# Attention over the tail of a KV cache on one core: unit 5's K is turned in later slots, and two weight loads change places

## The chip, the core and the metric

The kernel runs on one core of a Trainium2 chip. The core has engines that run side by side, each through its own instructions in order: TensorE (PE, with its weight loads shown apart as PEld), VectorE (DVE), ScalarE (ACT), GpSimd (POOL) and SyncE (SP), which here issues the loads. An instruction that needs another engine's result waits for a semaphore, and everything behind it on the same engine waits too. The metric is the device time of one execution in microseconds.

## The reference

Eight sequences, each with 32 new positions, 32 query heads and 4 KV heads. Of the cache only the last W = 2048 positions are used.

```python
W = min(4096, max(256, Sk // 4))          # Sk = 8192, so W = 2048
q = (x @ wq).reshape(B, Sq, Hq, Dh).transpose(0, 2, 1, 3)
k = jnp.repeat(k_cache[:, :, Sk - W:, :], rep, axis=1)
v = jnp.repeat(v_cache[:, :, Sk - W:, :], rep, axis=1)
p = softmax(einsum("bhqd,bhkd->bhqk", q, k) * Dh ** -0.5)
o = einsum("bhqk,bhkd->bhqd", p, v)
return o.transpose(0, 2, 1, 3).reshape(B, Sq, Hq * Dh) @ wo
```

x is 8 x 32 x 1024, wq 1024 x 4096, wo 4096 x 1024, a head is 128 wide; all is bfloat16.

## The kernel before

**Units and slots.** The work is cut into 32 units, one for each pair of KV head (group g) and sequence b, eight units to a group, in the order of the groups. A unit has 2048 keys and 256 query rows (8 heads x 32 positions). It is done in four chunks of 512 keys, and a chunk of a unit is a *slot*: unit 0 has slots 0 to 3, unit 5 has slots 20 to 23, and so on to slot 127. The loop in `run` (L452 to L485) writes into every engine's queue, slot by slot: the scores S = K Q^T of this chunk on PE (L464), the exponential on ACT (L466), the product P·V of the chunk two slots earlier on PE (L475), then side work. At the end of a unit `finish_unit` divides by the row sums and turns the result, on DVE (L412 to L419). At a unit's start DVE copies the loaded V into one of three tiles va whose rows hold V and a column of ones (L406); P·V reads that tile. The order is written by hand: each engine runs its instructions as they are emitted, and no scheduler moves them.

**Three ways to K^T.** PE needs K with the head dimension on the partitions. Units 0 to 4 (`PE_T`): K is loaded as it is, PE transposes it (L231, two pieces to a half, in the four slots of the unit before) and DVE copies each half out of PSUM (L233). Units 5, 8, 11, ... 29 (`V_T`): K is loaded as it is; DVE transposes 32 x 32 blocks of it into a tile kb, in four instructions (L246, "blocks"), and sixteen moves put the quarters in their places in kTv. POOL makes the moves (L256); for unit 5 one in four is made by DVE (L254). A move takes one 32-partition quarter of kb over all sixteen key tiles, so it needs all four blocks, and the scores need all sixteen moves. All other units: the DMA transposes on the way in (L193).

**Side work and its slots.** `side_plan` (L423) makes a list of pieces for each slot: the projections of Q for the next groups (`Q_SLOTS`, L270), the output projection (`O_SLOTS`, L290), and blocks and moves of the `V_T` units. An entry of `V_T` names the unit after whose loads K is loaded, the slots of the blocks, the first slot of the moves, the slot that they end before, and how many of sixteen moves are POOL's. `spread` deals pieces evenly over a range of slots. In a slot these pieces come last, after the copies of K_T pieces.

**Loads.** SP issues them in one queue. Units 2 and 3 are loaded in `start`, units 4 to 7 in slot 8, and unit u from 8 on in slot 4(u-5). `load_unit` (L202) issues K and V of a unit, then K of a `V_T` unit that is due there, and then the weights whose entry in `W_AT` names the unit. The weights are a list of 28 half-pieces of 512 KB; its first four are wq of group 1 (two halves of two), numbers 4 to 7 are wq of group 2. Eight loads can be on their way at a time: the next waits for the one eight places before it.

Of the kernel before, what the change touches and what calls it, by code (L numbers as in the profile page):

```python
# [21 lines left out]

PE_T = (0, 1, 2, 3, 4)

V_T = {5: (2, (5, 6, 8, 10), 10, 17, 12),
       **{u: (u - 4, range(4 * u - 16, 4 * u - 12), 4 * u - 13, 4 * u - 4, 16) for u in (8, 11, 14, 17, 20, 23, 26, 29)}}
W_AT = (3, 3, 4, 4, 8, 8, 9, 9, 11, 12, 13, 13, 14, 15, 16, 16, 18, 19, 19, 20, 22, 22, 23, 24, 25, 26, 28, 28)

Q_SLOTS = {1: (17, 31), 2: (38, 54), 3: (69, 83)}
O_SLOTS = {0: (54, 71), 1: (84, 101), 2: (99, 123), 3: (124, 143)}  # L30
# [71 lines left out]
class Fast:  # L102
# [72 lines left out]
    def load_k(self, ui, part=None):  # L175
# [3 lines left out]
        src = self.k_cache[b, g, self.Sk - self.W:, :]  # L179
        if ui not in V_T and ui not in self.kT:  # L180
            self.kT[ui] = self.ktp.tile([P, KT, P], BF16, name="kT")
        if ui in PE_T or ui in V_T:
            H = KT // 2
# [18 lines left out]
    def load_unit(self, ui):  # L202

        if ui < len(self.units):
            if ui not in V_T:
                self.load_k(ui, None if ui in PE_T else 0)
            self.load_v(ui, self.nc.sync)
            if ui not in V_T and ui not in PE_T:
                self.load_k(ui, 1)
        for u, at in V_T.items():  # L210
            if at[0] == ui:
                self.load_k(u)
        for p, at in zip(self.weights, W_AT):
            if at == ui:
# [21 lines left out]
    def kv_pieces(self, ui):  # L236
# [11 lines left out]
        def move(k, d):  # L248
# [3 lines left out]
            in_ = st["kb"][k * 32:(k + 1) * 32, :, d * 32:(d + 1) * 32]  # L252
            if d >= V_T[ui][4] // 4:
                nc.vector.tensor_copy(out=out, in_=in_)  # L254
# [168 lines left out]
    def side_plan(self):  # L423

        S = self.B * self.NCH
        plan = {s: [] for s in range((len(self.units) + 8) * self.NCH)}

        def spread(pieces, s0, s1):
            for k, p in enumerate(pieces):
                plan[s0 + (s1 - s0) * k // len(pieces)].append(p)  # L430
        for g, w in Q_SLOTS.items():
            spread(self.q_pieces(g), *w)
        for g, w in O_SLOTS.items():
            spread(self.o_pieces(g, 0) + (self.o_pieces(g, 1) if g < self.Hkv - 1 else []), *w)
        for ui, (_, s0, s1, s2, _) in V_T.items():
            blocks, moves = self.kv_pieces(ui)
            for k, p in enumerate(blocks):
                plan[s0[k]].append(p)
            spread(moves, s1, s2)
        return plan  # L440

# [209 lines left out]
```

## Time and profile before

| | us |
|---|---|
| median of 3 runs | 187.37 (187.13 to 187.44) |
| the profiled execution | 187.37 |
| its span, first to last instruction | 185.6 |
| PE busy in it | 178.8 |
| DVE busy | 115.1 |
| ACT busy | 131.7 |
| POOL busy | 94.7 |

The span is 1.77 us shorter than the time of the execution it belongs to. A row of a timeline has the start in us, the length in us, the engine, the line of the kernel, the operation, output and inputs with their shapes, and how many such instructions are merged; idle time of the engine before the row stands in brackets, with what ended it. Rows of one engine can overlap a little, since an instruction starts before the last has left the pipeline. A list of waits has who waited and for whom, the total in us, how many times, and the longest. A busy engine isn't by itself the bound: what counts is whose work is late for another.

The first loads reach PE at 4.3 us (x) and 6.8 us (the first weights of wq). Slot 4 starts at 18.98 us, slot 8 at 23.44, slot 12 at 27.89, slot 16 at 32.34, slot 20 at 37.65.

### The profile page before, as it was taken

What the parts mean: (1) busy time and instruction counts of PE and PEld (TensorE: products, weight loads), DVE (VectorE), ACT (ScalarE), POOL (GpSimd) and SP (SyncE); (2) the same over time, 40 slices, a digit from 0 to 9 for tenths busy, and PEclk for the clock granted to TensorE, in tenths of its full rate; (3) what the DMA queues carried; (4) which work ended last, traced back from release to release, by engine and by line L of the source; (5) the groups of instructions that cost most, each with busy time, mean ns of one, the idle gap of its engine ahead of it and who ended that gap; (6) DMA issues with size and microseconds to landing.
All of it is one profiled execution on the core that took longest, in us unless ns stands there. A gap on an engine that the chain in (4) does not pass through costs nothing. (4 is left out here: it accounts for less than half of the span.)

```text
span 185.6 us, 5054 instructions
## 1 busy us (share of the span) xinstructions
PE 178.8 (96%) x2048; PEld 153.1 (82%) x2064; DVE 115.1 (62%) x267; ACT 131.7 (71%) x133; POOL 94.7 (51%) x150
## 2 busy tenths in 40 slices
PE   7699999999999999999999999999999999999993
PEld 2589999999999999987878999987777888888842
DVE  0128699994586685586467558647746855445372
ACT  2207899787789777777777677787777888888700
POOL 2000007949939959929954980796299189500000
PEclk9999999999999999999999999999999999999999
DMA  6999999999999999999999999999999999930012
GB/s 151 321 397 415 414 415 389 195 270 353 296 274 304 310 320 398 368 240 254 376 323 250 367 349 276 202 409 357 269 371 329 192 326 174 276 96 0 4 62 62
DMA packets 52507, 51.75 MB, mean 279 GB/s; under 512 B 39424, under 2 KB 40064, under 8 KB 52480
## 3 DMA queue, kind: packets, MB, share of 16 engines
q1 hardware_dynamic: 51904, 50.87, 95.6%
q10 hardware_dynamic: 576, 0.52, 0.8%
q8 instruction: 17, 0.28, 0.6%
q14 instruction: 10, 0.08, 0.2%
HBM read 41.42 MB, written 0.52 MB: 226 GB/s over the span
## 5 line engine op out<-in xcount | busy, mean ns | idle before, releaser
L466 ACT ACTIVATE pT<-s_ps 128x1024 bf16<-128x1024 f32 x128 | 128.9, 1025 | 33.3 <-PE s_ps L464 32.3
L256 POOL TENSOR_SCALAR kTv<-kb 32x512 bf16<-32x512 bf16 x140 | 93.7, 670 | 65.4 <-DMA k_raw<-in_k_cache_dram 27.0
L475 PEld LDWEIGHTS <-pT 128*128 128x128 bf16 x1024 | 68.5, 98 | 3.1
L464 PEld LDWEIGHTS <-kT 128*128 128x128 bf16 x368 | 34.8, 98 | 10.3
L290 PE MATMUL op_ps<-wo_sb,OT 128*128 128x512 bf16 (+1 forms) x120 | 32.8, 365 | 0.8
L270 PE MATMUL q_ps<-xT,wq_sb 128*128 128x256 bf16 x192 | 28.2, 273 | 0.0
L475 PE MATMUL o_ps<-va_112,pT 128*128 128x129 bf16 x352 | 27.1, 220 | 0.0
L475 PE MATMUL o_ps<-va_113,pT 128*128 128x129 bf16 x352 | 27.0, 220 | 0.1
L475 PE MATMUL o_ps<-va_114,pT 128*128 128x129 bf16 x320 | 24.7, 220 | 0.0
L246 DVE STREAM_TRANSPOSE kb<-k_raw 128x512 bf16<-128x512 bf16 x36 | 23.8, 684 | 0.0
L412 DVE RECIPROCAL RL_all<-o_ps 128x2 f32<-128x2 f32 x32 | 5.2, 164 | 27.5 <-PE o_ps L475 27.5
L417 DVE TENSOR_SCALAR o_sb<-o_ps,RL_all 128x128 bf16<-128x128 f32 x64 | 19.5, 346 | 1.1
L464 PEld LDWEIGHTS <-kTv 128*128 128x128 bf16 x144 | 13.9, 98 | 5.1
L270 PEld LDWEIGHTS <-wq_sb 128*128 128x128 bf16 x192 | 17.0, 98 | 1.2
L464 PE MATMUL s_ps<-QT_63,kT 128*128 128x256 bf16 x112 | 16.8, 273 | 0.0
L419 DVE STREAM_TRANSPOSE OT<-o_sb 128x256 bf16<-128x256 bf16 x32 | 14.2, 445 | 1.1
L464 PE MATMUL s_ps<-QT_66,kT 128*128 128x256 bf16 x96 | 14.4, 273 | 0.1
L290 PEld LDWEIGHTS <-OT 128*128 128x128 bf16 x136 | 11.1, 98 | 2.8 <-DVEq L77 0.6
L464 PE MATMUL s_ps<-QT_65,kT 128*128 128x256 bf16 x80 | 12.0, 273 | 0.1
L464 PE MATMUL s_ps<-QT_64,kT 128*128 128x256 bf16 x80 | 12.0, 272 | 0.1
L297 DVE TENSOR_TENSOR oacc<-op_ps,oacc 128x512 f32<-128x512 f32 x8 | 5.5, 682 | 7.4 <-PE op_ps L290 7.4
L406 DVE COPY va_113<-v_sb 128x2048 bf16<-128x2048 bf16 x11 | 9.5, 859 | 0.0
(46 smaller groups left out, 104.0 us busy)
## 6 DMA issues: line engine op xcount, KB each, us to landing
v_sb<-in_v_cache_dram SPq DMA_DIRECT2D x32, 512.0 KB, 7.0
wo_sb<-in_wo_dram SPq DMA_DIRECT2D x16, 512.0 KB, 6.3
wq_sb<-in_wq_dram SPq DMA_DIRECT2D x14, 512.0 KB, 7.1
k_raw<-in_k_cache_dram SPq DMA_DIRECT2D x13, 512.0 KB, 5.7
wq_sb<-in_wq_dram SPq DMA_DIRECT2D x4, 256.0 KB, 7.0
kT<-in_k_cache_dram SPq DMA_TRANSPOSE x36, 6.9
k_raw<-in_k_cache_dram SPq DMA_DIRECT2D x2, 256.0 KB, 8.2
x_sb<-in_x_dram ACTq DMA_DIRECT2D x1, 256.0 KB, 3.7
```

The costliest lines, as they stand in the source:

```text
L246: nc.vector.transpose(out=st["kb"][:, sl, :], in_=self.k_raw[ui][:, sl, :])
L256: nc.gpsimd.tensor_scalar(out=out, in0=in_, scalar1=1.0, scalar2=1.0, op0=ALU.mult, op1=ALU.mult)
L270: nc.tensor.matmul(st["ps"][:, 0:self.NQ], lhsT=self.wq_t[g, i][:, c % (DC // 2), hl * P:(hl + 1) * P], rhs=self.xT[:, c, :], start=(c == ...
L290: nc.tensor.matmul(ps[:, 0:w], lhsT=self.OT[:, gq, c, t * P:(t + 1) * P], rhs=self.wo_t[gq][:, c, n0:n0 + w], start=(k == 0), stop=(k == 7))
L297: nc.vector.tensor_tensor(out=acc, in0=ps[:, 0:w], in1=acc, op=ALU.add)
L406: self.nc.vector.tensor_copy(out=self.va[ui % 3][:, :, 0:self.Dh], in_=self.v_sb[ui][:, :, :])
L412: nc.vector.reciprocal(out=rl[:, ui * QT_N:(ui + 1) * QT_N], in_=o_ps[:, :, Dh])
L417: nc.vector.tensor_scalar(out=o_sb[:, qt, :, :], in0=o_ps[:, qt, 0:Dh].rearrange("p (i c) -> p c i", c=4), scalar1=rl[:, ui * QT_N + qt:ui ...
L419: nc.vector.transpose(out=self.OT[:, g * QT_N:(g + 1) * QT_N, :, b * self.Sq:(b + 1) * self.Sq], in_=o_sb[:, :, :, :])
L464: nc.tensor.matmul(s_ps[:, jj, :], lhsT=self.kT[ui][:, c * CJ + jj, :], rhs=q_u, start=True, stop=True)
L466: nc.scalar.activation(out=pT[:, :, :], in_=s_ps[:, :, :], func=ACT.Exp, bias=0.0, scale=self.scale)
L475: nc.tensor.matmul(o_ps[:, qt, 0:self.VW], lhsT=pT[:, jj, qt * P:(qt + 1) * P], rhs=va[:, j, 0:self.VW], start=(j == 0 and qt == 0), stop= ...
```

## The change

`V_T` gets a range of slots for the blocks in place of a list, in the entry of unit 5 with other numbers. The blocks of unit 5 stood in slots 5, 6, 8 and 10; `spread(blocks, 6, 14)` puts them into 6, 8, 10 and 12. Its moves stood in slots 10 to 16 and now stand in 12 to 16. For the other units of `V_T`, `spread` gives the slots that stood there before. In `W_AT` the first entry goes from 3 to 2, so the first half-piece of wq of group 1 is issued behind K and V of unit 2 and K of unit 5, ahead of K and V of unit 3; and the eighth goes from 9 to 10, so the last half-piece of wq of group 2 is issued behind the loads of unit 10 and K of unit 14.

```diff
-V_T = {5: (2, (5, 6, 8, 10), 10, 17, 12),
-       **{u: (u - 4, range(4 * u - 16, 4 * u - 12), 4 * u - 13, 4 * u - 4, 16) for u in (8, 11, 14, 17, 20, 23, 26, 29)}}
-W_AT = (3, 3, 4, 4, 8, 8, 9, 9, 11, 12, 13, 13, 14, 15, 16, 16, 18, 19, 19, 20, 22, 22, 23, 24, 25, 26, 28, 28)
+V_T = {5: (2, 6, 12, 17, 12),
+       **{u: (u - 4, 4 * u - 16, 4 * u - 13, 4 * u - 4, 16) for u in (8, 11, 14, 17, 20, 23, 26, 29)}}
+W_AT = (2, 3, 4, 4, 8, 8, 9, 10, 11, 12, 13, 13, 14, 15, 16, 16, 18, 19, 19, 20, 22, 22, 23, 24, 25, 26, 28, 28)
@@ side_plan
         for ui, (_, s0, s1, s2, _) in V_T.items():
             blocks, moves = self.kv_pieces(ui)
-            for k, p in enumerate(blocks):
-                plan[s0[k]].append(p)
+            spread(blocks, s0, s1 + (s1 - s0) // 3)
             spread(moves, s1, s2)
```

The rows of V with their ones column are 320 bytes in both kernels (`VA_ROW` = 160).

## The prediction

> **What bounds the kernel now.** I read the page's totals and clock first, then PE's list of waits, then the engines' rows in order of time around the work that the change moves.
>
> ```profile
> PE 178.8 (96%) x2048; PEld 153.1 (82%) x2064; DVE 115.1 (62%) x267; ACT 131.7 (71%) x133; POOL 94.7 (51%) x150
> ...
> PEclk9999999999999999999999999999999999999999
> ...
> PE q_ps L372 <- DMA wq_sb<-in_wq_dram: 1.4, 1, 1.4
> ```
>
> PE is busy for 96% of the span at full clock. Its list of waits has one wait for loaded data, 1.4 us for the first weights, before 7 us. In its rows in order of time no group from 13.65 us to 180 us has idle time before it. So an engine that gets faster in between brings nothing, and only a new hole in PE can change the time there. The question is which results reach PE with little to spare. Unit 5's K^T is one: its scores are PE's first work on a turned K, in slot 20.
>
> ```profile
> 28.59 8.78 POOL L256 TENSOR_SCALAR kTv<-kb 32x512 bf16<-32x512 bf16 x12 [27.02 <-DMA k_raw<-in_k_cache_dram]
> ...
> 37.16 0.37 PEld L270 LDWEIGHTS <-wq_sb 128*128 128x128 bf16 x4
> 37.54 0.43 PEld L464 LDWEIGHTS <-kTv 128*128 128x128 bf16 x4
> ```
>
> POOL makes its twelve moves of unit 5 in one run from 28.59 to 37.37 us. PE loads the first weights from the result at 37.54. The slack is 0.17 us. The idle time before POOL's run is put down to a DMA, but K of unit 5 had landed at 20.94; what came last was the fourth block of L246 on DVE, since every move reads all sixteen tiles of kb:
>
> ```profile
> 22.98 1.28 DVE L246 STREAM_TRANSPOSE kb<-k_raw 128x512 bf16<-128x512 bf16 x2
> 24.19 0.65 DVE L233 COPY kT<-tp 128x1024 bf16<-128x1024 bf16 x1
> 24.77 0.67 DVE L406 COPY va_114<-v_sb 128x2048 bf16<-128x2048 bf16 x1
> 25.36 0.70 DVE L246 STREAM_TRANSPOSE kb<-k_raw 128x512 bf16<-128x512 bf16 x1
> ...
> 27.16 0.65 DVE L233 COPY kT<-tp 128x1024 bf16<-128x1024 bf16 x1
> 27.74 0.69 DVE L246 STREAM_TRANSPOSE kb<-k_raw 128x512 bf16<-128x512 bf16 x1
> 28.35 0.65 DVE L233 COPY kT<-tp 128x1024 bf16<-128x1024 bf16 x1
> 29.03 0.31 DVE L254 COPY kTv<-kb 32x512 bf16<-32x512 bf16 x1
> 29.38 1.04 DVE L406 COPY va_112<-v_sb 128x2048 bf16<-128x2048 bf16 x1
> ```
>
> The fourth block ends at 28.43 and POOL starts 0.16 later. DVE has no idle time from 22.4 to 41.9 us in this listing, so the place of a block in its queue is the time at which it is done.
>
> **The change, part 1: blocks and moves of unit 5.** The blocks go from slots 5, 6, 8, 10 to 6, 8, 10, 12; the moves from slots 10 to 16 into 12 to 16. Nothing is added or removed: four blocks, twelve moves on POOL, four on DVE. In the built program PE's, ACT's and POOL's orders are the same; on DVE the fourth block now stands behind the second kT copy of unit 3 and behind the V copy of unit 3 (va_112), and one move follows it. I walk DVE's queue again with the distances from start to start of the rows above: kT copy 0.58, block 0.62, V copy 0.59.
> - First block 22.98. The second kT copy of unit 2 would start at 23.60, but its transposes on PE end then (23.21 + 0.39), so 23.64; V copy 24.22; second block 24.81 to 25.43.
> - Unit 1's division waits for PE's last product at 25.61, so it starts at 25.65 (25.98 before). Its four instructions take 1.18 (25.98 to 27.16), so the first kT copy of unit 3 is at 26.83, the third block at 27.41.
> - The second kT copy of unit 3 waits for PE's transposes, which end at 28.06: 28.10. V copy of unit 3 28.68. Fourth block 29.27 to 29.96.
> - POOL starts at 29.96 + 0.16 = 30.12, 1.53 later than before.
>
> How long POOL's run takes: an undisturbed move lasts 0.61 with 0.06 before the next, so 12 x 0.61 + 11 x 0.06 = 8.0. Before, 8.78 were taken: one move lasted 0.96 beside the V copy of unit 3, one 0.95 beside that of unit 4 (at 33.89), one 0.70 beside a move on DVE. The first of these is gone, since that copy now lies before POOL's start; the other two stay: 8.0 + 0.34 + 0.09 = 8.45, and the end is 38.57. How soon PE follows POOL no row shows. The nearest is PE behind DVE at the start: the zeroed tile is done at 1.14, the first weight load at 1.19, so 0.05; from DVE to POOL it was 0.16. I take 0.05, the row that ends at PE. The load of unit 5's first K^T goes from 37.54 to 38.62: **a hole of 1.08 us in PE**, 1.53 less the slack of 0.17, less some 0.33 by which POOL's run is shorter, plus the 0.05. PE runs in order, and behind the waiting load stand the P·V of unit 4, Q pieces of group 1 and all later units. They have nothing spare to make it up with, so it stays to the end.
>
> Bounds: POOL undisturbed from 30.0 gives 38.0 and a hole of 0.5; POOL from 30.4 (DVE 0.3 late) with 8.78 and a further 0.3 from DVE's moves gives 39.5 and a hole of 2.0. A gain from this part is excluded: the fourth block can't stand before 29.2, because the kT copy ahead of it waits for PE's transposes.
>
> [...] The row: the V copy of unit 4 alone takes 0.67 (as at 24.77) and lengthened the move beside it by 0.34, not by its whole length. [...] I go by the row.
>
> What else DVE serves in this stretch: the kT copy of unit 4 ends at 32.19 and PE uses it at 32.23. In the new order unit 2's division stands behind the fourth block and one move: 29.96 + 0.03 + 0.31 + 0.04 = 30.34, as before (30.34). At 0.1 late, PE would wait that 0.1 in slot 16 and as much less in slot 20, so it adds nothing. V copy of unit 4: done 34.88, needed 35.44. The first block of unit 8 keeps its place, and POOL's run for unit 8 starts after that unit's fourth block (39.86), after the new end of unit 5's run.
>
> **Part 2: weights.** (a) The first half-piece of group 1's wq goes ahead of K and V of unit 3 in SP's queue, 512 KB. The transfers there land every 1.23 us (K of unit 3 22.16, V 23.40, weights 24.63), so K of unit 3 lands at 23.4 and V at 24.6. PE's transposes of it start at 24.33 with their weight load at 24.23: 0.8 spare where 2.1 were. V of unit 3 is read at 28.7. Cost 0; without the cover, 0.1 for every 0.1 beyond 24.2. Behind them the second half lands where it did, at 26.25. (b) The last half-piece of group 2's wq moves from behind unit 9's K, V to behind unit 10's K, V and K of unit 14. Before it landed at 56.05; the new place in the same queue, filled by the same bytes, is that of K of unit 14, 61.03. SP passes it over a transposing load (the DMA that SP was busy with until 56.03), so the transfers of unit 10 start one transfer sooner. PE reads this half first in slot 39, at 61.25, its third matmul 61.47, which the hole moves to 62.55. Cost 0 with 1.5 spare; bounds 0, and 0.9 if it lands only where the second transfer after it did (63.44).
>
> **Sum.** The profiled execution took 187.37 (span 185.6 and 1.77 around it), which is the median too. 187.37 + 1.08 + 0 + 0 = 188.45.
>
> **Rivals.**
> - The weights of group 2 come late as well. For: DMA falls to 10 to 34 GB/s for about a microsecond near 54.5 us while transposing loads run, and such a dip may now lie just before this half-piece. Against: the queue holds the same bytes. 188.45 + 0.9 = 189.35.
> [...]
> - Not slower: POOL's run fits after all. It would have to end by 37.49, 7.37 after its start, which is the twelve moves at their minimum of 0.607 (7.28) with no pauses. Then PE has no hole: 187.37. Against: pauses of 0.06 stand between all its moves now. It decides only from 0.6 us per move. A real gain would have to come from the first 13 us, where the order of loads is unchanged.
>
> **Chances.** Forecast 0.73, late weights 0.10, longer POOL run 0.08, POOL fits 0.09. The likeliest gives 188.45. The range goes from the lower bound of the hole (0.5, 187.9, less 0.1 for scatter) to the dearer rivals: 187.8 to 189.4. A measurement of this kernel tells about 0.2% (0.37 us) from no change; a hole of 0.5 is above that, so slower takes all but the last case: 0.91, with 0.07 for same and 0.02 for faster.
>
> **What would show it.** Right: POOL's run of twelve starts near 30.1 and ends near 38.6; PE's weight load of kTv in slot 20 waits for POOL about 1.1 us and is the only new wait; the span is some 186.7. Wrong: the run ends before 37.5; a wait of PE on k_raw near 24.2 or on wq_sb near 62; or a slot 20 without a hole and another time nevertheless.

## The result and the profile after

| | before | changed |
|---|---|---|
| median, us | 187.25 (187.13 to 187.44, 6 runs) | 188.31 (187.87 to 188.78, 6 runs) |
| ratio | | 1.0058, 95% interval 1.0041 to 1.0076 |
| the profiled execution, its span | 187.37, 185.6 | 188.31, 186.4 |

The change makes the kernel slower by 1.06 us. The changed kernel's rows around slot 20 show where. First POOL's run of moves for unit 5, then PE's weight loads (start, length, engine, line; in brackets the idle time before):

```profile
30.04 8.37 POOL L256 TENSOR_SCALAR kTv<-kb 32x512 bf16<-32x512 bf16 x12 [28.47 <-PE o_ps L474]
```

```profile
37.03 0.37 PEld L270 LDWEIGHTS <-wq_sb 128*128 128x128 bf16 x4
38.47 0.33 PEld L463 LDWEIGHTS <-kTv 128*128 128x128 bf16 x4 [1.06 <-POOL kTv L256]
```

(Lines of `run` are one less than before: L463 is the scores, L474 is P·V.) POOL starts 1.45 us later than before, its run ends at 38.41, and PE's weight load on kTv, which stood 0.01 us behind the last load on wq before, now stands idle for 1.06 us and starts 0.06 after POOL's end. DVE's rows show why POOL starts so late:

```profile
27.31 0.69 DVE L246 STREAM_TRANSPOSE kb<-k_raw 128x512 bf16<-128x512 bf16 x1
27.97 0.69 DVE L233 COPY kT<-tp 128x1024 bf16<-128x1024 bf16 x1
28.58 0.68 DVE L406 COPY va_112<-v_sb 128x2048 bf16<-128x2048 bf16 x1
29.18 0.70 DVE L246 STREAM_TRANSPOSE kb<-k_raw 128x512 bf16<-128x512 bf16 x1
29.91 0.29 DVE L254 COPY kTv<-kb 32x512 bf16<-32x512 bf16 x1
```

The fourth block stands behind the kT copy and the V copy of unit 3 and ends at 29.88. The bracket of POOL's row names P·V on PE as the releaser, but the block's end is 0.16 before POOL's start, the same distance as before. The V copy takes 0.68 here and took 1.04 before, when POOL's moves ran beside it.

From slot 20 on PE runs without new waits. The list of what its weight loads waited for has one entry that before lacks:

```profile
PEld L463 <- POOL kTv L256: 1.1, 1, 1.1
```

The first scores of unit 5 start 1.05 after the matmul ahead of them, where 0.11 is normal, so PE lost 0.94. From these scores to the last instruction both profiles take 147.9 us, so the loss stays whole. The changed execution had come through its start 0.12 faster (slot 16 at 32.22 against 32.34), which is why the spans differ by 0.8.

### The profile page after: what moved, and what is told of

Read it like the earlier page. It is cut to its first block, busy times and chain, and to the rows that moved or that the text cites. A ratio compares the mean times of both kernels' runs of the same rounds, so it can differ in the third digit from the quotient of the medians.

```text
span 186.4 us, 5054 instructions
## 1 busy us (share of the span) xinstructions
PE 179.0 (96%) x2048; PEld 152.9 (82%) x2064; DVE 116.0 (62%) x267; ACT 131.8 (71%) x133; POOL 94.2 (51%) x150
## 5 line engine op out<-in xcount | busy, mean ns | idle before, releaser
L465 ACT ACTIVATE pT<-s_ps 128x1024 bf16<-128x1024 f32 x128 | 129.0, 1025 | 34.2 <-PE s_ps L463 33.2
L474 PEld LDWEIGHTS <-pT 128*128 128x128 bf16 x1024 | 68.5, 98 | 3.1
L463 PEld LDWEIGHTS <-kT 128*128 128x128 bf16 x368 | 34.8, 98 | 10.3
L474 PE MATMUL o_ps<-va_112,pT 128*128 128x129 bf16 x352 | 27.1, 220 | 0.0
L474 PE MATMUL o_ps<-va_113,pT 128*128 128x129 bf16 x352 | 27.0, 220 | 0.1
L474 PE MATMUL o_ps<-va_114,pT 128*128 128x129 bf16 x320 | 24.7, 220 | 0.0
L463 PEld LDWEIGHTS <-kTv 128*128 128x128 bf16 x144 | 13.8, 98 | 6.2 <-POOL kTv L256 1.1
L463 PE MATMUL s_ps<-QT_63,kT 128*128 128x256 bf16 x112 | 16.8, 273 | 0.0
L463 PE MATMUL s_ps<-QT_66,kT 128*128 128x256 bf16 x96 | 14.4, 273 | 0.1
L463 PE MATMUL s_ps<-QT_65,kT 128*128 128x256 bf16 x80 | 12.0, 273 | 0.1
L463 PE MATMUL s_ps<-QT_64,kT 128*128 128x256 bf16 x80 | 12.0, 272 | 0.1
```

What stands on the lines that cost most here:

```text
L463: nc.tensor.matmul(s_ps[:, jj, :], lhsT=self.kT[ui][:, c * CJ + jj, :], rhs=q_u, start=True, stop=True)
L465: nc.scalar.activation(out=pT[:, :, :], in_=s_ps[:, :, :], func=ACT.Exp, bias=0.0, scale=self.scale)
L474: nc.tensor.matmul(o_ps[:, qt, 0:self.VW], lhsT=pT[:, jj, qt * P:(qt + 1) * P], rhs=va[:, j, 0:self.VW], start=(j == 0 and qt == 0), stop= ...
```

## The experiments

Each kernel is compared with runs of the kernel before on the same chip, whose medians were 187.29 (25 runs), 187.38 (11) and 187.43 (23) in the three groups. "Lost" is the distance from start to start across a hole, less the normal 0.11 us, or less 0.06 ahead of transposes.

**The parts by themselves.** The turn alone:

```diff
-V_T = {5: (2, (5, 6, 8, 10), 10, 17, 12),
+V_T = {5: (2, (6, 8, 10, 12), 12, 17, 12),
```

> The kernel before with the turn of unit 5 alone moved (blocks in slots 6, 8, 10, 12, moves in 12 to 16); the weights stay. Theory (the hole in PE comes from POOL's later run alone): POOL's run starts near 30.1 us against 28.6 and ends near 38.4; PE's first weight load of kTv waits some 1.0 us for it; 0.9 to 1.1 us slower than before, the whole of the change. Rival (the weights bear a part): no more than 0.5 us slower. Second question, the scatter: the changed kernel spread over 0.9 us in six runs, before over 0.3. If the turn makes it, these runs spread over 0.6 us or more.

188.39 us (187.96 to 188.89), ratio 1.005 (1.0033 to 1.0067): the whole of the change. POOL's run is that of the changed kernel to 0.01 us:

```profile
30.04 8.36 POOL L256 TENSOR_SCALAR kTv<-kb 32x512 bf16<-32x512 bf16 x12 [28.47 <-PE o_ps L475]
```

The second question fell away: on this chip the kernel before spread from 186.89 to 187.94 itself, so the scatter isn't the change's.

The weights alone:

```diff
-W_AT = (3, 3, 4, 4, 8, 8, 9, 9, ...
+W_AT = (2, 3, 4, 4, 8, 8, 9, 10, ...
```

> The kernel before with the two weight loads alone moved. Theory: K of unit 3 lands near 23.1 to 23.4 us, still ahead of its transposes at 24.2; the last half-piece of group 2's weights lands near 60 to 61, ahead of slot 39 at 61.2 to 61.5; no wait of PE is new; within 0.15 us of before. Rival (the weights bear a part): 0.3 to 0.6 us slower, with a wait of PE on k_raw near 24.2 or on wq_sb near 61. Scatter: if the weights make it, these runs spread over 0.6 us or more.

187.53 us, ratio 1.0012 (0.9996 to 1.0027), not told from no change by the times. The profile says more. PE's weight loads in slot 8:

```profile
23.89 0.23 PEld L231 LDWEIGHTS <-k_raw 128*128 128x128 bf16 x4 [0.17 <-DMA k_raw<-in_k_cache_dram]
```

K of unit 3 landed at 23.84, and PE lost 0.16. PE's rows in slot 39, where the second half of group 2's wq is first read:

```profile
60.82 0.38 PE L270 MATMUL q_ps<-xT,wq_sb 128*128 128x256 bf16 x2
61.55 0.39 PE L270 MATMUL q_ps<-xT,wq_sb 128*128 128x256 bf16 x2 [0.34 <-DMA wq_sb<-in_wq_dram]
```

The last half-piece landed at 61.50, and PE waited between the second and third matmul of the piece, losing 0.5. So the first theory, no new wait, was wrong in two places: with no hole in slot 20, the late weights do hold PE up in this execution. It had come through its start faster than the profile of before and would have read this half at 61.04, against 61.47 there; at the pace of before a landing at 61.50 would have cost 0.1 at most (an estimate from these times). In the changed kernel the last half-piece did not hold PE up: it landed at 60.11, and PE needed it at 62.29.

**What starts POOL.** Moves later, blocks as before:

```diff
-V_T = {5: (2, (5, 6, 8, 10), 10, 17, 12),
+V_T = {5: (2, (5, 6, 8, 10), 12, 17, 12),
```

> The kernel before with the moves of unit 5 in slots 12 to 16 and the blocks left in 5, 6, 8, 10. Theory (POOL's run is released by the fourth block, not by the slot in which its moves stand): POOL still starts near 28.6 and ends before 37.5, no hole, within 0.15 us of before; on DVE one move goes behind the V copy of unit 3 instead of ahead of it. Rival (the slots of the moves set POOL's start): a start near 30 and 0.5 to 1.1 us slower.

187.51 us, ratio 1.0005 (0.999 to 1.0019). POOL's row:

```profile
28.20 8.69 POOL L256 TENSOR_SCALAR kTv<-kb 32x512 bf16<-32x512 bf16 x12 [26.63 <-DMA k_raw<-in_k_cache_dram]
```

POOL starts at 28.20, 0.17 after the fourth block, though its moves stand two slots later in the plan. The rival falls: the blocks' place sets the start, the moves' slots don't. (PE loses 0.25 in another place, a P·V at 40.68 behind the V copy of unit 5, 40.63 at its end: DVE too is just in time.)

A larger dose, the fourth block one slot later still:

```diff
-V_T = {5: (2, (5, 6, 8, 10), 10, 17, 12),
+V_T = {5: (2, (6, 8, 10, 13), 13, 17, 12),
```

> The kernel before with blocks in slots 6, 8, 10, 13 and moves from slot 13: one slot later still, and on DVE behind unit 2's division and the first kT copy of unit 4. Theory (each us of POOL's start past the slack is a us of the run): the fourth block ends near 32.5, POOL runs from 32.7 to 41.1, the hole in PE is 3.6 us and the kernel 3.4 to 3.8 us slower than before. Rival (part of a hole is made good later by PE): clearly less, under 2.5 us. A third possibility is a lower granted clock after so long a hole, which would make it more than 4 us.

192.23 us, ratio 1.024 (1.0205 to 1.0275), but in two groups. The profiled execution took 190.79, 3.5 us more than before, and its PE rows hold all of it:

```profile
35.75 0.61 PE L475 MATMUL o_ps<-va,pT 128*128 128x129 bf16 x8 [0.39 <-DVE va L406]
...
40.93 0.61 PE L464 MATMUL s_ps<-QT,kTv 128*128 128x256 bf16 x4 [2.80 <-POOL kTv L256]
```

POOL started at 32.51. PE lost 0.55 behind DVE's V copy of unit 4, which the block had pushed back, and 2.97 behind POOL: 3.52 together. Nothing of it is made good later: from the first scores of unit 5 to the last instruction it is 148.0 us here and 147.9 before. The rival falls. Of the six executions two had a mean granted clock of 1.000 and took 190.45 and 190.79; four had 0.991 and took 192.01 to 192.62. That is the third possibility of the expectation, in most executions but not all; the profile is of one without it. More on it below.

**Is POOL's run the price?** The changed kernel with two of POOL's twelve moves on ACT:

```diff
+            if ui == 5 and k == 3 and d in (1, 2):
+                nc.scalar.copy(out=out, in_=in_)
-            if d >= V_T[ui][4] // 4:
+            elif d >= V_T[ui][4] // 4:
```

> The changed kernel with two of POOL's twelve moves of unit 5, of the last group, on ACT. Theory (the hole is POOL's start plus the length of POOL's run): POOL still starts near 30.05, makes ten moves and ends near 37.0, ahead of PE's need at 37.4; no wait of PE on kTv; 0.7 to 1.1 us of the change's loss comes back, within 0.3 us of before. Rival (the late weights or DVE hold PE up next): a hole of 0.3 us or more in another place and 0.5 us or more slower than before.

187.66 us, ratio 1.001 (0.9999 to 1.0021): the loss of about 1 us is gone. POOL's run and PE's loads in slot 20 (this kernel has two lines more: L258 is POOL's move, L465 the scores, L476 P·V):

```profile
30.07 7.01 POOL L258 TENSOR_SCALAR kTv<-kb 32x512 bf16<-32x512 bf16 x10 [28.51 <-PE o_ps L476]
```

```profile
37.17 0.37 PEld L272 LDWEIGHTS <-wq_sb 128*128 128x128 bf16 x4
37.55 0.42 PEld L465 LDWEIGHTS <-kTv 128*128 128x128 bf16 x4
```

POOL starts as late as in the change, ends at 37.08, and PE's load follows the one ahead of it with no gap. The other parts of the change are all still in this kernel. What is left are short holes: 0.32 at 24.23 on K of unit 3, 0.10 at 36.34 and 0.13 at 40.88. The first is the moved weight load at work, so the rival's hole of 0.3 is there, but not its 0.5 us: the medians differ by 0.23.

The changed kernel with four more of the moves on DVE:

```diff
-V_T = {5: (2, 6, 12, 17, 12),
+V_T = {5: (2, 6, 12, 17, 8),
```

> The changed kernel with eight of unit 5's sixteen moves on DVE and eight on POOL (four and twelve in the change). Theory (DVE has as little to spare in this stretch as POOL): POOL ends near 35.8 us and no longer holds PE up in slot 20, but DVE does three more moves of 0.3 to 0.7 us ahead of the V copy of unit 4, which then ends near 36.5 to 37 where PE needs it at 35.3; the hole goes to the P V of slot 18 and is 1.2 to 1.9 us; 1.2 to 2.0 us slower than before, no faster than the change. Rival (POOL's load alone is what costs): the hole is gone and the time within 0.3 us of before.

188.64 us, ratio 1.007 (1.0057 to 1.0083). POOL is done early, and PE waits for DVE instead:

```profile
PE o_ps L474 <- DVE va L406: 0.6, 1, 0.6
PE s_ps L463 <- DVE kT L233: 0.4, 1, 0.4
```

It lost 0.50 at 32.69 (the kT copy of unit 4 came late), 0.72 at 36.51 (V copy of unit 4) and 0.26 at 42.07. No better than the change: in this stretch the same work is late whether POOL or DVE has it. On ACT it was not.

The kernel before with the same two moves on ACT:

> The kernel before with the same two moves on ACT: POOL's slack at slot 20 grows from 0.17 to some 1.5 us. Theory (PE has no hole there before, so there is nothing to win): within 0.15 us of before. Rival (in executions that were not profiled POOL is late before too): 0.2 us faster or more.

187.56 us, ratio 1.0006 (0.9995 to 1.0016). POOL's run ends at 36.17, against 37.37 before:

```profile
28.75 7.42 POOL L258 TENSOR_SCALAR kTv<-kb 32x512 bf16<-32x512 bf16 x10 [27.19 <-PE s_ps L466]
```

The rival falls: where PE has no hole, more slack for POOL is worth nothing. No version that was run is faster than the kernel before.

**How far the loads' covers reach.** Two half-pieces of weights ahead of K of unit 3, where the change puts one:

```diff
-W_AT = (3, 3, 4, 4, 8, 8, 9, 9, ...
+W_AT = (2, 2, 4, 4, 8, 8, 9, 9, ...
```

> The kernel before with both half-pieces of the first half of group 1's wq ahead of K and V of unit 3 (the change puts one there). Theory (K of unit 3 has 0.8 us to spare behind one): behind two it lands near 24.7 to 25.0 us, PE's transposes of unit 3 wait for it in slot 8, a hole of 0.4 to 0.9 us near 24.2, and the kernel is 0.3 to 0.9 us slower. Rival (loads of this stretch are early enough anyway): no wait on k_raw, within 0.15 us.

188.73 us, ratio 1.0076 (1.0053 to 1.0099). PE's weight loads in slot 8:

```profile
25.34 0.23 PEld L231 LDWEIGHTS <-k_raw 128*128 128x128 bf16 x4 [1.27 <-DMA k_raw<-in_k_cache_dram]
```

K of unit 3 landed at 25.30, 0.3 to 0.6 later than I had expected, and PE lost 1.25. So the price of a second half-piece was put too low. And one can already be too much: with one ahead, PE lost 0.16 on K of unit 3 with the weights alone, 0.32 with two moves on ACT, and 0.19 in the changed kernel run again (below); in two other profiles it lost nothing.

The last half-piece of group 2's wq behind unit 11's V, with the turn as before, and then with the turn as in the change:

```diff
-W_AT = (3, 3, 4, 4, 8, 8, 9, 9, ...
+W_AT = (3, 3, 4, 4, 8, 8, 9, 11, ...
```

> The kernel before with the last half-piece of group 2's wq behind unit 11's V (the change has it one unit sooner, behind unit 10). Theory (it is the landing of this half that slot 39 waits for): it lands near 62.3 to 63, PE needs it at 61.0 to 61.5, a hole of 1.0 to 1.9 us, the kernel 0.8 to 1.8 us slower than before. Rival (the hole seen at 61.5 with the weights alone moved was chance): a hole under 0.3 us.

> As the run before it, and the turn of unit 5 moved as in the change. Theory (loads go their own pace, so the hole of 0.95 us in slot 20 puts slot 39 off by as much and is taken off the wait there): a hole of 0.9 to 1.0 in slot 20 and what is left of the other in slot 39, 0 to 0.9; the time within 0.4 us of the run before it. Rival (the two add up): 0.9 to 1.1 us slower than the run before it.

The first: 189.07 us (188.60 to 191.79), ratio 1.0107 (1.0067 to 1.0147; 191.79 is not in the ratio). The second: 189.56 us (188.76 to 190.78), ratio 1.0134 (1.0096 to 1.0173). The profile of the first is of its slowest execution. In it the half landed at 64.43, later than the 62.3 to 63 expected, and PE lost 3.02 in slot 39:

```profile
64.47 0.61 PE L270 MATMUL q_ps<-xT,wq_sb 128*128 128x256 bf16 x2 [2.86 <-DMA wq_sb<-in_wq_dram]
```

In the profile of the second it landed at 62.94, and PE lost 0.94 in slot 20 and 0.48 here:

```profile
62.29 0.38 PE L270 MATMUL q_ps<-xT,wq_sb 128*128 128x256 bf16 x2
62.98 0.39 PE L270 MATMUL q_ps<-xT,wq_sb 128*128 128x256 bf16 x2 [0.32 <-DMA wq_sb<-in_wq_dram]
```

The first theory holds: slot 39 waits for this half. Whether a hole in slot 20 takes as much off that wait is not settled cleanly: the medians differ by 0.5, between the two theories, and the landings of these two profiles lie 1.5 us apart, more than the 0.94 in question. The fastest of each are 188.60 and 188.76. Of the second's six executions three took 188.76 to 188.96 and three 190.16 to 190.78, all at a clock of 0.997 or more; what held up the latter no trace that is kept shows.

**The changed kernel again.**

> The changed kernel once more, on the chip of these runs. Theory: 0.9 to 1.2 us slower than before, a hole of 0.9 to 1.1 us at slot 20, no wait in slot 39, with the last half of group 2's weights landing 1 us or more ahead of PE's need. Rival (the profile of it was a lucky one): a second hole near 62 us and 1.3 us slower or more.

188.33 us, ratio 1.0053 (1.0033 to 1.0073). The hole in slot 20 is there again (0.94), with POOL from 30.08. Slot 39 has no wait, but the half landed at 61.55 and was needed at 62.33: 0.8 to spare, not 1 or more. And K of unit 3, landed at 24.19, held PE up, which neither theory nor rival had; PE lost 0.19:

```profile
24.23 0.23 PEld L231 LDWEIGHTS <-k_raw 128*128 128x128 bf16 x4 [0.20 <-DMA k_raw<-in_k_cache_dram]
```

## Why the prediction was right

Point by point, the prediction's number first and the changed kernel's profile second.

- *Nothing to win.* PE without a hole before: confirmed by ending POOL's run 1.2 us sooner (36.17 with two moves on ACT, 37.37 before), which brought nothing.
- *The fourth block.* Start 29.27, measured 29.18; POOL's start 30.12, measured 30.04. DVE's queue walked by start-to-start distances came out within 0.1 us over thirteen instructions, and moving the block another slot or moving the moves alone behaved as the same walk says. The walk was not carried on to the V copy of unit 4, for which the prediction kept the times of before (done 34.88, needed 35.44). In the change it is done at 35.25 and read at 35.31:

```profile
34.21 1.04 DVE L406 COPY va_113<-v_sb 128x2048 bf16<-128x2048 bf16 x1
```

```profile
35.31 0.62 PE L474 MATMUL o_ps<-va_113,pT 128*128 128x129 bf16 x8
```

So nothing of its slack was left. That this cost nothing was luck: in the larger dose the same copy cost 0.55.

- *POOL's run.* 8.45 (its terms add up to 8.43), measured 8.37; end 38.57 and 38.41. One of the two long moves that were expected is there (0.95, beside the V copy of unit 4); the other, 0.70 beside a move on DVE, isn't. The move beside the V copy took 0.34 longer than the 0.61 of an undisturbed one, as in the row of before, though that copy alone takes 0.67. The row of before held here, and the 8.37 decides: the longer run, to which the prediction gave 0.08, did not come.
- *The hole.* 1.08, measured 0.94. It was counted from weight load to weight load. After the wait, the first matmul starts together with its load at 38.47, where in a dense stretch it starts 0.11 behind it, so the matmuls lost 0.11 less than the loads. That the medians differ by 1.06, nearly the 1.08, is partly chance: the median of the kernel before alone lies between 187.25 and 187.43 in the four groups of runs.
- *It stays to the end.* From slot 20 to the end the change takes 147.9 us, as before, and the larger dose lost what its holes added up to, 3.5, in the execution that was profiled.
- *Weights at no cost.* Right in the sum, on thinner ground than the prediction said. K of unit 3 was given 0.8 to spare. In the two profiles of the changed kernel it had 1.1 (23.05 against a load at 24.15) and none, with 0.2 waited. A wait there is among the prediction's own signs of being wrong, so that the first profile had none was partly luck: of the five profiles with this load ahead of K of unit 3, three have one, of 0.16 to 0.32. The last half of group 2 was given 1.5 and had 2.2 and 0.8. Moved alone, it came 0.5 too late in its profile. The prediction took one execution's landings for fixed times, and that was the error; between the two profiles of the changed kernel they differ by 1.1 and 1.4 us.

The rival of late weights is no empty one: the wait showed as soon as the turn was put back, and with the weights one unit later it cost 1.7 us in the median. In the changed kernel the hole in slot 20 moves PE's need 0.94 later; that this is what covers it is argued from the landing times, not shown by a clean comparison, and in its first profile, with the half landed at 60.11, the cover was not needed. The rival that POOL's run might fit is out: it needed 7.37 us or less and took 8.37.

## What to carry to other kernels

Where the bounding engine has no hole, ask of each moved step only how much later its last result comes and how much slack stood ahead of the engine that reads it: here 1.45 us of delay met 0.17 us of slack. In an order written by hand, walk the queue of the engine that makes the *releasing* step and not the slots of the steps that follow it; the moves could go two slots later at no cost that the times tell, the block couldn't. A cover (the time by which a load is early) that is read from one profile is worth no more than the scatter of the landing, which between the two profiles of the changed kernel was 1.1 us for K of unit 3 and 1.4 us for the last half of group 2's wq.

## What the runs showed that I had not expected

One hole of 3.02 us cost more than itself. In the kernel with group 2's weights behind unit 11, the windows from the start of the 3.02 us hole on (stretch, length, busy time and count of each engine, granted clock, DMA share, GB/s) read:

```profile
61.62:63.84 2.22, 0.00 (x0) 0.00 (x0) 0.00 (x0) 0.44 (x1) 2.03 (x4) 1.00 0.98 335
63.84:64.47 0.63, 0.00 (x0) 0.00 (x1) 0.00 (x0) 0.00 (x0) 0.57 (x2) 0.50 2.55 138
64.47:67.25 2.78, 2.78 (x18) 2.22 (x19) 2.08 (x3) 1.02 (x1) 1.44 (x3) 0.50 0.84 243
67.25:68.00 0.75, 0.75 (x10) 0.69 (x9) 0.00 (x0) 0.00 (x0) 0.00 (x0) 1.00 1.16 300
```

PE's last matmul ended at 61.61. The clock fell to 0.50 at 63.84, inside the hole, and was whole again at 67.25, 3.41 us later. PE worked for 2.78 us of that, and a group of four score matmuls took 1.06 us where 0.60 is usual:

```profile
64.88 1.06 PE L464 MATMUL s_ps<-QT,kT 128*128 128x256 bf16 x4
```

That execution took 191.79, 4.4 more than before: the hole explains 3.0, and 2.78 us at half clock the other 1.4 (an estimate from these windows). In the kernel with the block in slot 13 the 2.97 us hole left the clock at 1.00 in the profiled execution, and four of the other five were some 1.8 us longer at a mean clock of 0.991, the mean of the execution above too. No trace of these four is kept, so that their clock fell in the same way is argued, not shown. The changed kernel's hole of 0.94 never showed it (mean clock 0.997 to 1.000 in its twelve executions). In the execution above the clock fell when PE had been idle for 2.23 us (61.61 to 63.84); in the profiled one with the block in slot 13 an idle time of 2.80 us left it whole. So these runs give no idle time at which it falls.
